# A one-core attention-and-MLP kernel: a quarter of w_out and one of w_in held behind a memset, six buffers for the last half tiles, and second stores right behind the first

## The chip, the cores and the metric

The kernel runs on one core of one Trainium2 chip. The metric is the device time of one execution in microseconds (us), the median over several runs. Before the change three runs gave 106.68, 106.97 and 108.76 us, median 106.97 us. Profiles come from one profiled execution each.

The engines are named as in the profile: PE (TensorE: matmuls; PEld is its weight load), DVE (VectorE), ACT (ScalarE), POOL (GpSimd) and SP (SyncE, which here only issues DMAs). SPq and ACTq are DMA issues on those two.

## The reference

An attention layer with polynomial sketch features is followed by a two-layer MLP with a PReLU that has one slope per hidden unit.

```python
def phi(x):                                   # 8 x 8 products of two 8-wide sketches
    a = np.einsum('rd,bhsd->bhsr', S1, x)
    b = np.einsum('rd,bhsd->bhsr', S2, x)
    return np.einsum('bhsi,bhsj->bhsij', a, b).reshape(*x.shape[:-1], r * r)
q_p, k_p = (phi(q), phi(k))
kv = np.einsum('bhsf,bhsd->bhfd', k_p, v)
z = np.sum(k_p, axis=2)
num = np.einsum('bhsf,bhfd->bhsd', q_p, kv)
den = np.einsum('bhsf,bhf->bhs', q_p, z)[..., None] + 1e-06
attn = num / den
x = attn.transpose(0, 2, 1, 3).reshape(B * S, H * D)
h = x @ w_in
out = (np.maximum(h, 0.0) + alpha * np.minimum(h, 0.0)) @ w_out
```

q, k and v are 4 batches x 4 heads x 1088 tokens x 32; r = 8; w_in is 128 x 2048, w_out 2048 x 128; the output is 4352 x 128, all float32.

## The kernel before, in words

The program is a graph of named operations that is written out in a fixed order. `Graph.build` makes the operations; the string `ORDER` lists them as `name@engine` (a, d, g, p, s for ACT, DVE, POOL, PE, SP), and every engine runs its own part of the list strictly in that order. The list `SLOTS` says which buffer of its class each temporary uses. No planner runs on the chip: an engine waits on semaphores for the data that its next instruction needs, and everything behind that instruction waits with it.

**Stages.** Loads bring q, k and v of the four batches and the weights in quarters (`w_in0`..`w_in3`, `w_out0`..`w_out3`, 256 KB each) into SBUF. For each batch the key side (`k{b}...`) builds features, products (`k0p00` and so on: batch 0, part 0 or 1, head 0 to 3) and the key-value matrix; the query side (`f0`, `f1` for the first 16 rows of batch 0, then `q0`..`q3`, `qr`) makes the normalised tokens x in bf16. The MLP then runs over tiles `0a`, `0b`, `1`..`9`: `h` is x @ w_in on PE into PSUM, `r` the ReLU on ACT or DVE, `o` the second matmul with `w_a` = (1 - alpha) w_out, and `W` adds x @ (w_in diag(alpha) w_out), because PReLU is (1 - alpha) ReLU(h) + alpha h.

**Weights.** From a quarter of w_out come `w_a{i}`, then `w_b{i}` (alpha times w_out, in one of two buffers, wb__111 and wb__112), then `w_hi{i}` and `w_lo{i}` (its bf16 head and rest). `Wmm` multiplies all of them with the transposed w_in on PE.

**Loads.** All large loads are issued by SP (line 143), in list order; a load that has to wait holds back those behind it. A `hold` operation (line 159) is a memset of one column of a load's destination: since the load writes the same column, its issue waits for the memset, which stands at a chosen place in another engine's order. There are eight DMA semaphores, used in turn, so a DMA also waits until the one eight places ahead of it has landed.

**The last tiles.** Tiles 1 to 6 hold 512 tokens; their result is transposed by DVE (`t1`..`t6`) into one of three oT buffers and leaves in two pairs of DMAs of 64 KB each (`s4.0`, `s4.1`). Tiles 7, 8 and 9 hold 256 tokens and end in halves a and b of 128: `t7a`..`t9b` copy PSUM to an oL buffer (ACT for the a halves, DVE for the b halves), and `s7a`..`s9b` store it from SP or ACT. All three a halves gather in the same PSUM bank, bank 7. The oL buffers are two tiles of their own (oL__101 and oL__102) and two old ones, E8 (printed as E) and kvF:

```python
T["oL"] += [T["E8"], T["kvF"]]
```

t7a and t8a use oL__101, t7b and t8b oL__102, t9b E8 and t9a kvF. The order of the last instructions is: `t8b` on DVE, then `t9b` on DVE; on ACT the issue of `s8a`, the issue of `s8b`, then `t9a` and the issue of `s9a`.

Of the kernel before, what the change touches and what calls it, by code (L numbers as in the profile page):

```python
# [42 lines left out]
class Graph:  # L43
# [106 lines left out]
    def loads(self):  # L150
        T = self.T
# [7 lines left out]
        hold = {n: self.op(f"hold.{n}", [("pool", 100, 140), ("dve", 60, 140)], lambda e, t=t: (self.nc.vector if e == "dve" else self.nc.gpsimd).memset(  # L159
            T[t][:, :1] if t != "q_r" else T[t][:, :1, :1], 0.0)) for n, t in (("k1", "k1"), ("q1", "q1"), ("k2", "k2"), ("q2", "q2"), ("qr", "q_r"))}  # L160
# [510 lines left out]
ld.k1.0@s f0.x@d q0cb@g vpad2@d fill@1 bit@2 h0a.6@p ld.k2.1@s f1.dT@d w_hi3@a ld.w_out2@s w_in_bf0@a h0a.4@p h0a.10@p r0a.6@a h0a.14@p w_lo3@g f1.e@a
k0W@a k1T0@d r0a.14@a w_b0@g winT0@p h0a.12@p q0s@d w_hi0@a winTc0@d f1.rc@d r0a.10@a q0e@a w_b2@g o0a.6@p k1f@p w_lo0@g winT1@p k1ab@d winTc1@d
w_hi2@a h0a.8@p h0a.2@p ld.q2.0@s ld.v3.3@s r0a.4@a r0a.8@a w_a0@a q0rc@d f1.num@p w_lo2@d q0bd@g f1.rr@d k1z@p r0a.12@d f1.x@d ld.q3.0@s ld.k2.0@s
q0p00@g q0p01@g k2T0@d h0a.0@p o0a.4@p Wmm@p h0b.4@p h0b.10@p r0a.0@a r0a.2@a o0a.0@p W_lo@a w_a2@g k1p01@g h0b.2@p W@d o0a.2@p W0a@p k1p00@g k1p03@g
k2f@p h0b.0@p o0a.8@p r0b.10@a q0t0@d k1zm@d w_a3@a o0a.10@p o0a.14@p r0b.0@a r0b.2@a k2ab@d ld.v2.1@s ld.qr@s ld.q1.0@s k1cw@p q0n@p q1T@d k1cc@d
q0x0@a q2T@d o0a.12@p h0b.12@p k2z@p t0a@d k2zm@d r0b.12@a r0b.4@a q1f@p h0b.14@p k1p02@g k2p00@g W0b@p o0b.2@p h1.6@p q1g@d q1cb@d ld.v1.1@s o0b.0@p
o0b.10@p h0b.6@p h1.13@p r0b.14@a r0b.6@a r1.6@a h1.9@p h1.5@p q1s@d k2p01@g ld.v1.2@s h0b.8@p h1.0@p ld.v1.3@s ld.v3.1@s ld.v2.3@s ld.v2.2@s
ld.v1.0@s q1e@g r0b.8@a o0b.4@p h1.10@p r1.5@a r1.9@a r1.10@a ld.v2.0@s ld.v3.0@s ld.k3.1@s h1.15@p r1.13@d q1rc@d h1.7@p o0b.14@p o0b.12@p h1.2@p
o0b.8@p h1.12@p r1.7@d k2p03@g q1bd@g o0b.6@p h1.4@p r1.2@d r1.15@a k2cw@p t0b@d k1v0@p k2cc@d r1.12@d r1.4@a q2f@p o1.12@p s0b.1@a k1vc@a h1.8@p
o1.5@p o1.4@p o1.6@p o1.15@p q1p00@g q1p01@g h1.3@p q2g@d W1@p h1.1@p o1.9@p h1.14@p r1.3@a q1p11@g k2p02@g ld.k3.0@s q1t0@d s0a.1@s h1.11@p k1vT@p  # L680
k2v0@p r1.0@a k1W@a r1.14@a k2vc@a r1.1@a q1p10@g q2cb@g o1.0@p o1.2@p q1t1@d r1.11@a k3T0@d r1.8@d q2s@d q2e@g o1.10@p o1.14@p o1.3@p o1.7@p q1n@p
q1x0@a k3f@p q2rc@d k3ab@d o1.8@p o1.1@p q1x2@a h2.6@p h2.8@p h2.11@p h2.2@p q2bd@g q2p00@g k3p01@g q2p01@g r2.8@a r2.6@a h2.3@p h2.0@p r2.3@a o1.13@p
o1.11@p h2.9@p r2.2@a r2.0@d t1@d h2.15@p k3z@p k2vT@p r2.9@d h2.14@p k3zm@d r2.14@d h3.10@p o2.2@p h2.1@p h3.2@p q2p11@g k3p00@g r2.11@a k2W@a qrT@d
r3.10@a q2p10@g k3p03@g r2.1@a r2.15@a h2.7@p o2.14@p h2.12@p o2.8@p h2.10@p h2.4@p o2.15@p o2.1@p ld.v3.2@s s1.1@s s0b.0@s r2.12@a r3.2@d o2.12@p
h3.3@p r2.4@a r2.10@a h3.13@p r2.7@a o2.9@p h2.13@p h2.5@p q3T@d o2.4@p o2.11@p o2.3@p h3.7@p W2@p h3.0@p o2.10@p q2t0@d h3.14@p r2.5@a r2.13@a r3.3@a
o2.13@p o2.6@p h3.11@p h3.9@p o2.0@p r3.13@d q2t1@d o2.5@p r3.7@a r3.0@a r3.9@a o2.7@p r3.14@a k3cw@p q2n@p t2@d r3.11@a k3cc@d q2x0@d q2x2@a h3.15@p
W3@p o3.14@p h3.5@p s1.0@s s0a.0@s q3f@p o3.3@p h4.14@p r3.15@d r3.5@a h3.6@p o3.10@p o3.11@p q3g@d o3.7@p h5.14@p h3.4@p o3.9@p h4.11@p h5.1@p q3cb@g
r3.4@a r4.14@d h3.8@p o3.5@p h4.1@p r5.1@a r4.11@a o3.0@p h3.1@p o3.13@p r3.6@d q3s@d r3.8@d q3e@g o3.2@p h3.12@p o3.4@p h4.9@p r3.12@a r5.14@d
k3p02@g r4.9@a r3.1@a h4.13@p h4.15@p q3rc@d o3.12@p o3.8@p o3.6@p h4.8@p h4.0@p o3.15@p h4.12@p h4.6@p o3.1@p r4.13@a q3bd@d r4.15@d t3@d r4.1@d
r4.8@a h4.2@p h4.7@p k3v0@p o4.9@p h4.4@p o4.1@p o4.15@p q3p11@g q3p10@g r4.7@a r4.2@a q3p00@d r4.4@a q3t1@d h5.3@p o4.8@p W4@p h5.13@p o4.4@p r4.12@a  # L690
k3vc@d q3p01@d r4.0@a h4.10@p h5.11@p o4.13@p h4.3@p o4.11@p r4.3@a o4.14@p o4.12@p r4.6@d q3t0@d h5.10@p h4.5@p o4.3@p o4.0@p r4.10@a r4.5@a s2.1@a
o4.7@p h5.5@p o4.2@p r5.10@d r5.13@d r5.5@d r5.3@a o4.6@p o4.5@p o4.10@p h5.15@p h5.6@p h5.4@p h5.2@p h5.9@p t4@d s2.0@s k3vT@p s4.1@s s3.1@s r5.9@d
r5.6@a r5.11@a r5.4@a o5.10@p o5.3@p o5.5@p o5.1@p k3W@d r5.15@d q3n@p q3x0@a h5.8@p h5.0@p r5.0@a o5.11@p q3x2@d o5.9@p qrf@p s3.0@a r5.8@a r5.2@d
qrg@d h6.6@p o5.6@p o5.15@p o5.0@p h5.12@p h5.7@p h6.10@p W5@p r5.7@d h6.5@p o5.4@p h6.9@p qrcb@g r5.12@d r6.9@d o5.7@p h6.15@p o5.13@p h6.12@p
o5.14@p o5.8@p r6.10@a r6.6@a qrs@d qre@d r6.15@a o5.12@p o5.2@p qrrc@d r6.12@d h6.2@p h6.3@p t5@d qrbd@g h6.14@p h6.13@p h8.12@p qrp00@g h6.1@p
r6.3@a r6.2@d r6.13@a r6.5@a o6.9@p o6.3@p h6.0@p o6.10@p s5.0@s r6.14@a r6.0@a o6.2@p h6.4@p h6.7@p o6.5@p o6.6@p r8.12@d qrt0@d r6.1@d o6.12@p qrn@p
qrx0@d o6.15@p h6.11@p r6.4@a o6.1@p h7.10@p h7.12@p h7.0@p h8.8@p r6.11@a r6.7@a o6.0@p h6.8@p r6.8@d r7.0@d o6.13@p r7.10@a o6.7@p h7.14@p h7.2@p
h7.4@p o7b.10@p W6@p r7.12@a o6.8@p o6.14@p o6.11@p o6.4@p r7.2@a r7.4@a o7b.4@p h8.2@p h9.10@p o7b.12@p r7.14@a t6@d r8.2@a h8.14@p h7.6@p r8.14@a
o7b.0@p h7.8@p s6.0@s o7a.12@p W7a@p o7a.10@p o7b.2@p o7a.4@p r7.8@d r8.8@d h9.8@p h8.0@p W7b@p o7a.2@p o7a.14@p r7.6@a o7a.6@p o7a.0@p o7a.8@p
o8b.8@p h9.2@p o8b.14@p h9.4@p r8.0@d r9.8@d t7a@a o8b.0@p o7b.8@p o7b.6@p h9.0@p o7b.14@p o8a.12@p r9.2@a s7a.0@s s4.0@s r9.10@d r9.0@d t7b@d W8a@p  # L700
h8.6@p o8a.14@p o8a.0@p h8.4@p r8.4@a s7b.0@s o8b.12@p h8.10@p r8.10@a h9.6@p W8b@p r9.4@a o8a.8@p o8b.2@p r8.6@d h9.12@p W9b@p o8a.2@p o8a.6@p
o8a.10@p o8a.4@p o8b.6@p o9b.8@p h9.14@p o9b.2@p s6.1@s s5.1@s r9.12@d t8a@a r9.6@a o9a.10@p o9a.8@p o9b.10@p o8b.4@p o9a.4@p W9a@p r9.14@d o9a.0@p
# [66 lines left out]
```

## Time and profile before

| what | value |
|---|---|
| runs (us) | 106.68, 106.97, 108.76; median 106.97 |
| profiled execution | 106.47 us; span 104.6 us from the first to the last instruction |
| granted TensorE clock | 0.991 |
| busy share: PE, DVE, ACT, POOL | 91%, 74%, 66%, 46% |
| data moved | 11.28 MB, HBM read 8.80 MB, written 2.23 MB |

A row of the chain of waits is a start, a length and what the time went to. A row of the timeline is a start, a length, the engine, the line of the kernel, the operation, output and inputs; xN merges N instructions, and a bracket gives the idle time of the engine before it and what ended that. A row of the windows gives a stretch, its length, and then busy time and instruction count for PE, PEld, DVE, ACT and POOL, the clock, the DMA engines' busy share and GB/s. L137 is the helper through which every matmul but the transposes is issued, and L134 the one for two-operand vector work, so tiles tell more than lines there.

### The profile page before, as it was taken

The numbers are of one execution on the slowest core, as the hardware profiler recorded it, in microseconds if no ns is written. First come the engines' busy times: TensorE is split into PE (matmuls) and PEld (weight loads), VectorE is DVE, ScalarE is ACT, GpSimd is POOL, SyncE is SP. The second block draws the span as 40 slices with busy tenths as digits, with TensorE's granted clock in tenths as the row PEclk, the third lists the DMA queues.
The fourth block names the chain that finished last, engine by engine and source line by source line (L and its number), as shares of the span: only waits on it lengthen the run. The fifth ranks groups of instructions, "written<-read, shape, count | busy, mean of one in ns | idle before, by whom it ended". The sixth has DMA issues, their size and how long they took to land.

```text
span 104.6 us, 3655 instructions
## 1 busy us (share of the span) xinstructions
PE 95.2 (91%) x1517; PEld 56.1 (54%) x1531; DVE 77.4 (74%) x149; ACT 68.5 (66%) x137; POOL 48.3 (46%) x65
## 2 busy tenths in 40 slices
PE   7998748999999999999999999999999999999920
PEld 2365626576766746444444444644534456699810
DVE  3589939999998686867986894999767963589510
ACT  3336994998769637479996279576566567855410
POOL 5169957989999996199910168000001500000000
PEclk9999999999999999999999999999999999999996
DMA  2997989999862100003502000002431020022362
GB/s 67 315 304 240 342 244 339 355 381 341 246 190 62 26 5 6 0 6 61 89 0 49 7 0 0 6 0 50 74 57 25 0 50 6 0 50 50 75 116 75
DMA packets 21730, 11.28 MB, mean 108 GB/s; under 512 B 16192, under 2 KB 19024, under 8 KB 21712
## 3 DMA queue, kind: packets, MB, share of 16 engines
q1 hardware_dynamic: 18552, 10.49, 34.9%
q10 hardware_dynamic: 3160, 0.54, 2.6%
q8 instruction: 12, 0.20, 0.8%
q14 instruction: 6, 0.05, 0.2%
HBM read 8.80 MB, written 2.23 MB: 105 GB/s over the span
## 4 chain that ended last, share of the span: by engine, by line
PE 75%; DMA 8%; SPq 5%; DVE 4%; issue 2%; ACT 2%; POOL 1%; ACTq 0%; DVEq 0%; POOLq 0%
PE ps L137 74%; DMA w_out_f<-in_moe_w_out_dram 5%; DMA out_dram<-oL__102 3%; SPq L578 3%; SPq L143 2%; POOL wb__112 L134 1%; DVE aq__82 L416 1%; DVE winT L124 1%; ACT w_hl L122 1%; DVE kp__70 L134 1%; DVE rh__91 L552 1%; ACT aq__82 L122 1%; PE ps L391 1%; DVE kvW L124 0%; ACTq L578 0%
## 5 line engine op out<-in xcount | busy, mean ns | idle before, releaser
L137 PE MATMUL ps<-xT__103,w_in_bf 128*128 128x512 bf16 (+1 forms) x111 | 28.0, 333 | 0.3 <-issue 0.2
L137 PEld LDWEIGHTS <-w_in_bf 128*128 128x128 bf16 x176 | 16.2, 98 | 12.6 <-issue 2.1
L137 PEld LDWEIGHTS <-w_a 128*128 128x128 bf16 x128 | 12.3, 98 | 12.6 <-issue 1.7
L137 PE MATMUL ps<-xT__104,w_in_bf 128*128 128x256 bf16 (+1 forms) x63 | 14.9, 326 | 0.1
L550 ACT ACTIVATE rh__88<-ps 128x512 bf16<-128x512 f32 x13 | 7.8, 597 | 7.0 <-PE ps L137 6.9
L550 ACT ACTIVATE rh__89<-ps 128x512 bf16<-128x512 f32 x15 | 9.0, 599 | 4.6 <-PE ps L137 4.6
L134 POOL TENSOR_TENSOR kp__69<-kab__66 128x576 f32<-128x576 f32 (+1 forms) x11 | 11.4, 1053 | 1.0 <-DVE kab__66 L333 0.9
L134 POOL TENSOR_TENSOR dn__80<-gt__73 128x128 f32<-128x128 f32 (+2 forms) x3 | 1.5, 498 | 22.0 <-DVE gt__73 L451 22.0
L550 ACT ACTIVATE rh__90<-ps 128x512 bf16<-128x512 f32 x12 | 7.1, 596 | 1.6 <-PE ps L137 1.1
L134 POOL TENSOR_TENSOR pr__75<-gt__73 128x512 f32<-128x512 f32 x7 | 7.3, 1068 | 0.7 <-DVE gt__73 L134 0.4
L323 DVE STREAM_TRANSPOSE kT__64<-k 128x1152 f32<-128x1152 f32 (+1 forms) x5 | 5.6, 1126 | 1.6 <-DMA k<-in_k_dram 1.4
L137 PE MATMUL ps<-const-bfloat16-1.0 128*128 128x512 bf16 (+1 forms) x20 | 5.8, 425 | 1.0 <-PEq L753 0.8
L137 PE MATMUL ps<-pt__78,kvW 32*32 32x256 f32 (+2 forms) x320 | 6.4, 332 | 0.1
L550 ACT ACTIVATE rh__92<-ps 128x512 bf16<-128x512 f32 x9 | 5.4, 602 | 1.3 <-PE ps L137 1.3
L552 DVE TENSOR_SCALAR rh__91<-ps 128x512 bf16<-128x512 f32 x7 | 4.7, 672 | 1.9 <-PE ps L137 1.6
L550 ACT ACTIVATE rh__93<-ps 128x512 bf16<-128x512 f32 x9 | 5.4, 601 | 0.8 <-PE ps L137 0.7
L550 ACT ACTIVATE rh__94<-ps 128x512 bf16<-128x512 f32 x9 | 5.4, 600 | 0.6 <-ACT rh__92 L550 0.4
L137 PE MATMUL ps<-rh__88,w_a 128*128 128x256 bf16 (+1 forms) x20 | 5.7, 326 | 0.1
L122 ACT CAST w_in_bf<-w_in_f 128x512 bf16<-128x512 f32 x4 | 4.5, 1122 | 1.7 <-DMA w_in_f<-in_moe_w_in_dram 1.7
L480 DVE STREAM_TRANSPOSE pt__78<-pr__75 128x1024 f32<-128x1024 f32 (+1 forms) x5 | 5.6, 1112 | 0.0
L137 PE MATMUL ps<-rh__89,w_a 128*128 128x512 bf16 (+1 forms) x16 | 5.3, 353 | 0.0
L137 PEld LDWEIGHTS ps<-pt__78,kvW 32*32 32x32 f32 x320 | 3.8, 103 | 2.3 <-DVE kvW L124 0.6
(199 smaller groups left out, 226.9 us busy)
## 6 DMA issues: line engine op xcount, KB each, us to landing
v<-in_v_dram SPq DMA_DIRECT2D x12, 144.0 KB, 3.9
q<-in_q_dram SPq DMA_DIRECT2D x3, 512.0 KB, 5.9
k<-in_k_dram SPq DMA_DIRECT2D x4, 288.0 KB, 4.5
k<-in_k_dram SPq DMA_DIRECT2D x4, 256.0 KB, 3.9
w_in_f<-in_moe_w_in_dram SPq DMA_DIRECT2D x4, 256.0 KB, 4.4
w_out_f<-in_moe_w_out_dram SPq DMA_DIRECT2D x4, 256.0 KB, 4.7
q<-in_q_dram SPq DMA_DIRECT2D x2, 256.0 KB, 4.2
out_dram<-oT__100 SPq DMA_DIRECT2D x8, 64.0 KB, 1.9
```

Of the source, the lines that this page charges most:

```text
L122: nc.scalar.copy(dst, src)
L124: (nc.vector if e == "dve" else nc.gpsimd).tensor_copy(dst, src)
L134: (self.nc.vector if e == "dve" else self.nc.gpsimd).tensor_tensor(out=dst, in0=a, in1=b, op=what)
L137: self.nc.tensor.matmul(out, w, x, start=start, stop=stop, skip_group_check=True)
L143: (self.nc.sync if eng == "sp" else self.nc.scalar).dma_start(dst(), src())
L323: turns.append(self.op(f"k{b}T{x}", [self.dvt(32 * NG * n)], lambda e, lo=lo, n=n: nc.vector.transpose(self.sb(bT, 32 * NG * lo, [1, 32 * ...
L391: nc.tensor.transpose(self.ps(bf4, 128 * f, [1, 128]), self.sb(bs4, 128 * f, [1, 128]), T["ident"])
L416: mu = self.op(f"f{u}.m", [self.dve(512)], lambda e, bp=bp, ba=ba: nc.vector.tensor_mul(self.sb(ba, 0, [128, 4], [1, 128]), self.ps(bp, 12 ...
L480: ts.append(self.op(f"{tag}t{x}", [self.dvt(64 * g)], lambda e, bP=bP, x=x: nc.vector.transpose(self.sb(bPT, 64 * g * x, [1, 64 * g]), sel ...
L550: nc.scalar.activation(self.sb(br), self.ps(bh, 0, [1, 512]), ACTF.Relu)
L552: nc.vector.tensor_scalar_max(self.sb(br), self.ps(bh, 0, [1, 512]), 0.0)
L578: (nc.scalar if e == "act" else nc.sync).dma_start(to(), at())
```

## The change

Four things are edited.

1. A new hold, `hold.wo`, clears one column of the fourth quarter of w_out (w_out_f3). It stands on POOL behind `k0p03`, and `ld.w_out3` depends on it.
2. In SP's order `ld.w_in1` goes ahead of `ld.w_out3`; `ld.w_in0` stays behind `ld.w_out3`, so it is held with it.
3. The class oL has six buffers instead of four: w_in_f0 and w_in_f1, whose contents were cast to bf16 near the start, join E8 and kvF. The slots of t8a, t8b, t9a, t9b move from oL__101, oL__102, kvF, E8 to E8, kvF, w_in_f0, w_in_f1. All six halves now have a buffer of their own.
4. The stores `s4.0`, `s5.1` and `s6.1` go directly behind `s4.1`, `s5.0` and `s6.0` on SP.

The diff, with the list of the order and the slots cut to the lines that carry this:

```diff
-               "rh": 10, "oT": 3, "oL": 4, "xT": 4, "zm": 2, "fs": 2, "wb": 2}
+               "rh": 10, "oT": 3, "oL": 6, "xT": 4, "zm": 2, "fs": 2, "wb": 2}
...
-            T[t][:, :1] if t != "q_r" else T[t][:, :1, :1], 0.0)) for n, t in (("k1", "k1"), ("q1", "q1"), ("k2", "k2"), ("q2", "q2"), ("qr", "q_r"))}
+            T[t][:, :1] if t not in ("q_r", "w_out_f3") else T[t][:, :1, :1], 0.0)) for n, t in (("k1", "k1"), ("q1", "q1"), ("k2", "k2"), ("q2", "q2"), ("qr", "q_r"), ("wo", "w_out_f3"))}
...
-                             lambda: self.dram("moe_w_out", 512 * i * DM, [512, 128], [1, 512]), 1 << 18, rate=420)
+                             lambda: self.dram("moe_w_out", 512 * i * DM, [512, 128], [1, 512]), 1 << 18, rate=420, deps=[hold["wo"]] if i == 3 else ())
...
-    T["oL"] += [T["E8"], T["kvF"]]
+    T["oL"] += [T["E8"], T["kvF"], T["w_in_f0"], T["w_in_f1"]]
...
-         4, 1, 6, 9, 2, 6, 3, 2, 1, 9, 6, 2, 7, 0, 5, 1, 0, 3, 3, 7, 2, 8, 0, 0, 6, 4, 4, 5, 4, 6, 6, 9, 7, 3, 1, 2]
+         4, 1, 6, 9, 2, 6, 3, 2, 1, 9, 6, 2, 7, 2, 5, 3, 0, 3, 3, 7, 2, 8, 0, 0, 6, 4, 4, 5, 4, 6, 6, 9, 7, 4, 1, 5]
```

SP's loads near the start, before (-) and now (+); w_in_f_150 to w_in_f_152 are w_in0 to w_in2, w_out_f_157 is w_out3, q_144 the second half of batch 0's q, and k_142 the second part of batch 1's k.

```order
 L143 DMA w_in_f_152<-in_moe_w_in_dram 128x512
 L143 DMA q_144<-in_q_dram 128x512
+L143 DMA w_in_f_151<-in_moe_w_in_dram 128x512
 L143 DMA w_out_f_157<-in_moe_w_out_dram 128x512
-L143 DMA w_in_f_151<-in_moe_w_in_dram 128x512
 L143 DMA w_in_f_150<-in_moe_w_in_dram 128x512
 L143 DMA k_142<-in_k_dram 128x512
```

w_in1 has moved ahead of w_out3; w_out3 now also waits for POOL, and w_in0 and the k load stand behind it as before.

SP's stores at the end, before (-) and now (+); oT__100, oT__98 and oT__99 hold tiles 4, 5 and 6, oL__101 and oL__102 the halves 7a and 7b.

```order
-L578 DMA out_dram<-oT__100 32x16x32 x2
-L578 DMA out_dram<-oT__98 32x16x32 x4
-L578 DMA out_dram<-oT__99 32x16x32 x2
+L578 DMA out_dram<-oT__100 32x16x32 x4
+L578 DMA out_dram<-oT__98 32x16x32 x6
+L578 DMA out_dram<-oT__99 32x16x32 x4
 L578 DMA out_dram<-oL__101 32x2x128 x2
-L578 DMA out_dram<-oT__100 32x16x32 x2
 L578 DMA out_dram<-oL__102 32x2x128 x2
-L578 DMA out_dram<-oT__99 32x16x32 x2
-L578 DMA out_dram<-oT__98 32x16x32 x2
```

The three late pairs, one between the stores of 7a and 7b and two behind them, have moved ahead of both.

ACT's last instructions, before (-) and now (+): the copies t8a and t9a (L122), the last ReLU of an even half tile (L550), and the issues of s8a, s8b and s9a (L578); E_128 is E8, w_in_f_150 is w_in_f0.

```order
 L550 ACTIVATE rh__90<-ps 128x512
 L550 ACTIVATE rh__96<-ps 128x512
-L122 COPY oL__101<-ps 128x128
+L122 COPY E_128<-ps 128x128
 L550 ACTIVATE rh__88<-ps 128x512
-L578 DMA out_dram<-oL__101 32x4x128
-L578 DMA out_dram<-oL__102 32x4x128
-L122 COPY kvF<-ps 128x128
+L578 DMA out_dram<-E_128 32x4x128
 L578 DMA out_dram<-kvF 32x4x128
+L122 COPY w_in_f_150<-ps 128x128
+L578 DMA out_dram<-w_in_f_150 32x4x128
```

The instructions and their order are the same; only the buffers differ, so t8a no longer writes the tile that s7a reads. On DVE the two last copies, t8b and t9b, likewise go to kvF and w_in_f1 instead of oL__102 and E8. PE's instructions are unchanged, and POOL has one memset more.

More of the change, by code (lines that the diff above doesn't have):

```diff
@@ L671 @@
[L671 to L702, printed above, removed]
@@ L703 @@
-o8b.10@p t8b@d o9b.0@p o9a.12@p o9b.14@p o9b.12@p o9b.4@p o9b.6@p s8a.0@a t9b@d s8b.0@a o9a.6@p s9b.0@s o9a.2@p o9a.14@p t9a@a s9a.0@a
+alphaT@d f0.a@p f0.b@p k0fz@p k0cw@p k0p00@g f0.ac@a w_a1@a w_in_bf2@a k0p10@d k0p03@g hold.wo@g f0.m@d fill@3 f1.a@p k0p02@d f1.b@p k0p13@g k0p12@g
+k0v0@p k0v1@p k0zz@d vpad1@d f1.ac@a k0cc@d kpad1@d k0zc@d k0Vc@a w_b1@g k0vc@a f0.den@p fill@1 k0VT@p ld.q0.1@s q0T1@d f1.m@d f0.dT@d hold.q2@d
+w_hi1@a f0.e@a k0V@d q0f@p ld.w_in1@s ld.w_out3@s k0vT@p f0.num@p f0.rc@d w_b3@g q0g@d ld.w_in0@s ld.k1.1@s ld.w_out0@s w_lo1@g f0.rr@d w_in_bf1@a
@@ new lines @@
+f1.den@p ld.k1.0@s f0.x@d q0cb@g vpad2@d fill@1 bit@2 h0a.6@p ld.k2.1@s f1.dT@d w_hi3@a ld.w_out2@s w_in_bf0@a h0a.4@p h0a.10@p r0a.6@a h0a.14@p
+w_lo3@g f1.e@a k0W@a k1T0@d r0a.14@a w_b0@g winT0@p h0a.12@p q0s@d w_hi0@a winTc0@d f1.rc@d r0a.10@a q0e@a w_b2@g o0a.6@p k1f@p w_lo0@g winT1@p k1ab@d
+winTc1@d w_hi2@a h0a.8@p h0a.2@p ld.q2.0@s ld.v3.3@s r0a.4@a r0a.8@a w_a0@a q0rc@d f1.num@p w_lo2@d q0bd@g f1.rr@d k1z@p r0a.12@d f1.x@d ld.q3.0@s
+ld.k2.0@s q0p00@g q0p01@g k2T0@d h0a.0@p o0a.4@p Wmm@p h0b.4@p h0b.10@p r0a.0@a r0a.2@a o0a.0@p W_lo@a w_a2@g k1p01@g h0b.2@p W@d o0a.2@p W0a@p
@@ new lines @@
+r8.2@a h8.14@p h7.6@p r8.14@a o7b.0@p h7.8@p s6.0@s s6.1@s o7a.12@p W7a@p o7a.10@p o7b.2@p o7a.4@p r7.8@d r8.8@d h9.8@p h8.0@p W7b@p o7a.2@p o7a.14@p
+r7.6@a o7a.6@p o7a.0@p o7a.8@p o8b.8@p h9.2@p o8b.14@p h9.4@p r8.0@d r9.8@d t7a@a o8b.0@p o7b.8@p o7b.6@p h9.0@p o7b.14@p o8a.12@p r9.2@a s7a.0@s
+r9.10@d r9.0@d t7b@d W8a@p h8.6@p o8a.14@p o8a.0@p h8.4@p r8.4@a s7b.0@s o8b.12@p h8.10@p r8.10@a h9.6@p W8b@p r9.4@a o8a.8@p o8b.2@p r8.6@d h9.12@p
+W9b@p o8a.2@p o8a.6@p o8a.10@p o8a.4@p o8b.6@p o9b.8@p h9.14@p o9b.2@p r9.12@d t8a@a r9.6@a o9a.10@p o9a.8@p o9b.10@p o8b.4@p o9a.4@p W9a@p r9.14@d
@@ L704 @@
+o9a.0@p o8b.10@p t8b@d o9b.0@p o9a.12@p o9b.14@p o9b.12@p o9b.4@p o9b.6@p s8a.0@a t9b@d s8b.0@a o9a.6@p s9b.0@s o9a.2@p o9a.14@p t9a@a s9a.0@a
 """
```

27 lines of the change are left out of this document (24 added, 3 removed).

## The prediction

> **What bounds the kernel now.** I read the page first, then the windows, the chain of waits, and the timeline at both ends.
>
> ```profile
> span 104.6 us, 3655 instructions
> PE 95.2 (91%) x1517; PEld 56.1 (54%) x1531; DVE 77.4 (74%) x149; ACT 68.5 (66%) x137; POOL 48.3 (46%) x65
> ```
>
> PE is idle for 104.6 - 95.2 = 9.4 us. The windows (stretch, length, then busy time and instructions of PE, PEld, DVE, ACT, POOL) tell where.
>
> ```profile
> 10.28:12.52 2.24, 2.21 (x120) 1.78 (x121) 1.98 (x8) 2.24 (x6) 2.24 (x4) 1.00 1.04 370
> 12.52:14.48 1.96, 0.00 (x0) 0.00 (x0) 0.80 (x3) 1.89 (x5) 1.95 (x2) 1.00 0.87 271
> 26.00:90.00 64.00, 63.17 (x967) 33.66 (x978) 50.13 (x82) 44.69 (x87) 29.06 (x32) 1.00 0.19 42
> ```
>
> From 26 to 90 us PE is idle for 0.83 us of 64, and its instructions don't change. An edit can gain there only by reaching those 0.83 us; what it can gain besides lies at the two ends. One hole at the start is 1.96 us in which PE does nothing at all. The chain, at the start and at the end:
>
> ```profile
> 13.90 5.02 DMA w_out_f<-in_moe_w_out_dram
> ...
> 19.05 1.05 POOL wb__112 L134
> ...
> 21.46 9.65 PE ps L137 x196
> ...
> 97.31 3.13 DMA out_dram<-oL__102
> ...
> 100.51 0.29 DVE oL__102 L124
> ...
> 101.43 0.27 ACT kvF L122
> ```
>
> The start hangs, by this chain, on a quarter of w_out that lands at 13.90 + 5.02 = 18.92 us. The end hangs on a store: the DMA that reads oL__102 (s7b) lands at 97.31 + 3.13 = 100.44, and 0.07 us later DVE copies the next half, t8b, into the same buffer. That is the place where the change takes something away for certain.
>
> **The end: six buffers.** PE's last matmuls, the first rows for the wait before 97.95:
>
> ```profile
> 97.54 0.28 PE L137 MATMUL ps<-w_a,rh__95 128*128 128x128 bf16 x2
> 97.95 0.27 PE L137 MATMUL ps<-w_a,rh__93 128*128 128x128 bf16 x2
> ...
> 98.67 0.28 PE L137 MATMUL ps<-w_a,rh__90 128*128 128x128 bf16 x2
> ...
> 99.34 0.39 PE L137 MATMUL ps<-w_a,rh__88 128*128 128x128 bf16 x4
> ...
> 99.68 0.28 PE L137 MATMUL ps<-w_a,rh__97 128*128 128x128 bf16 x2
> ```
>
> By the written order the 98.67 row is o8b.10, the last matmul of half 8b; the 99.34 row holds o9b.6, the last of 9b; the 99.68 row is o9a.14, the last of all. What ACT and DVE then do:
>
> ```profile
> 97.63 0.27 ACT L122 COPY oL__101<-ps 128x128 f32<-128x128 f32 x1 [0.34 <-ACT rh__96 L550]
> ...
> 97.93 0.66 ACTq L578 DMA_DIRECT2D out_dram<-oL__101  x1
> 100.84 0.55 ACTq L578 DMA_DIRECT2D out_dram<-oL__102  x1
> 101.43 0.27 ACT L122 COPY kvF<-ps 128x128 f32<-128x128 f32 x1 [3.03 <-DVE E L124]
> 101.72 0.55 ACTq L578 DMA_DIRECT2D out_dram<-kvF  x1
> ```
>
> ```profile
> 100.51 0.29 DVE L124 COPY oL__102<-ps 128x128 f32<-128x128 f32 x1 [2.09 <-DMA out_dram<-oL__102]
> 100.72 0.28 DVE L124 COPY E<-ps 128x128 f32<-128x128 f32 x1
> ```
>
> Half 8b is ready at 98.67 + 0.28 = 98.95, but t8b starts at 100.51. Behind it wait t9b on DVE and, on ACT, the issue of s8b (100.84) and t9a (101.43), which stands behind that issue though PE had finished at 99.68 + 0.28 = 99.96.
>
> With its own buffer t8b runs at 98.95 + 0.07 = 99.02 (the 0.07 as between the store's landing and t8b in the chain) to 99.31. s8b is issued 0.04 later, as before (100.80 to 100.84), and takes 0.55: 99.90. t9a needs ACT and PE: 99.90 + 0.04 or 99.96 + 0.07 = 100.03, so 100.03 instead of 101.43, a gain of 1.40 us. The issue of s9a keeps its distance of 0.29 to t9a. t9b needs the 99.34 row, whose end is 99.73 at the latest: 99.80 to 100.08 and its store is issued by SP ahead of s9a. What is late next is PE itself.
>
> A smaller term: PE stands still from 97.54 + 0.28 = 97.82 to 97.95. The matmul at 97.95 opens half 9a in bank 7, which t8a empties until 97.90. t8a had ACT idle for 0.34 us before it; in the order it waits for the two stores of s7a, since it writes oL__101. It now writes E8 and can start at 97.29, so these 0.13 us of PE go too, and all that follows moves. If ACT had waited there for something else, this term is nothing. Sum at the end: 1.40 + 0.13 = 1.53 us. The last store itself should land as fast:
>
> ```profile
> out_dram<-kvF ACTq DMA_DIRECT2D x1, 64.0 KB, 1.9
> ```
>
> **The stores that move.** On SP these stood between and behind the stores of tile 7:
>
> ```profile
> 95.08 1.13 SPq L578 DMA_DIRECT2D out_dram<-oT__100  x2
> 96.72 1.45 SPq L578 DMA_DIRECT2D out_dram<-oL__102  x2
> ```
>
> Without the first pair s7b is issued earlier, but with six buffers nobody waits for s7b any more, so I count no second gain. The pairs now go out before 94 us, while PE has work that no store feeds: about 1.1 us of SP each, SP idle otherwise. Cost and gain nothing. If this cover fails, s7a is issued up to 1.1 us later, and that only reaches t8a through a buffer that it no longer uses.
>
> **The start: the held loads.**
>
> ```profile
> 7.41 0.43 SPq L143 DMA_DIRECT2D w_out_f<-in_moe_w_out_dram  x1
> 7.89 0.90 SPq L143 DMA_DIRECT2D w_in_f<-in_moe_w_in_dram  x2
> 11.37 0.33 SPq L143 DMA_DIRECT2D k<-in_k_dram  x1
> ```
>
> ```profile
> 1.32 0.10 POOL L159 MEMSET q_r<- 128x1 f32 x1
> ...
> 8.05 1.86 POOL L134 TENSOR_TENSOR kp__70<-kab__66 128x320 f32<-128x320 f32 x2
> ...
> 12.29 1.04 POOL L134 TENSOR_TENSOR wb__112<-w_out_f,alphaT 128x512 f32<-128x512 f32 x1
> 13.34 1.16 POOL L134 TENSOR_TENSOR w_hl<-wb__111,w_hl 128x512 bf16<-128x512 f32 x1
> 16.23 0.46 POOL L134 TENSOR_TENSOR dn__80<-gt__73 128x128 f32<-128x128 f32 x1 [1.73 <-DVE gt__73 L451]
> ```
>
> The memset is POOL's next instruction behind the two kp__70 products, which end at 8.05 + 1.86 = 9.91. Like the memset at 1.32 it takes at most 0.10 us, so w_out3 is issued at about 10.0 instead of 7.41 and w_in0 at about 10.5; w_in1 takes the place at 7.41. Both issues end by 10.9, and the next load, k of batch 1, was issued only at 11.37, so SP's later loads keep their times. The 0.10 us on POOL are covered by the 1.73 us of idle time before 16.23; without that cover they cost 0.10.
>
> When does w_out3 land? The nearest rows, for the first load (an empty queue) and for the slowest quarter of w_out:
>
> ```profile
> k<-in_k_dram SPq DMA_DIRECT2D x1, 288.0 KB, 2.9
> ...
> w_out_f<-in_moe_w_out_dram SPq DMA_DIRECT2D x1, 256.0 KB, 5.0
> ```
>
> So between 12.9 and 15.0. Its first user is w_b3, the 12.29 row; behind it on POOL are w_lo1 (1.16) and then a wait for DVE until 16.23. w_b3 and w_lo1 need 1.04 + 1.16 = 2.20 us, so a landing until 16.23 - 2.20 = 14.0 costs nothing. I take about 13.3, nearer to the empty queue, because the two loads ahead of it (q and w_in1) were issued over 2 us before. On ACT:
>
> ```profile
> 14.44 0.62 ACT L122 CAST w_hl<-wb__112 128x512 bf16<-128x512 f32 x1
> ...
> 17.47 0.60 ACT L550 ACTIVATE rh__88<-ps 128x512 bf16<-128x512 f32 x1 [1.39 <-PE ps L137]
> ```
>
> w_hi3 at 14.44 needs w_b3, which ends at 13.3 + 1.04 = 14.34: nothing. At 15.0 it would slip to 16.1, by 1.7 us, with w_in_bf0 and the first ReLU behind it; 1.39 us are covered by ACT's idle time before 17.47, leaving 0.3. POOL would be 15.0 - 14.0 = 1.0 us late. So the hold's cost lies between nothing and 1.0. The other way, no load ahead of it waits behind it, so w_in1 alone is earlier, and nothing waited for w_in1. I take zero.
>
> The Trainium skill, "DMA: Bandwidth & Descriptors", section Rules for kernel authors, says to issue a DMA early and wait for it late; by that rule the hold gives away 2.6 us of cover and is a loss. The trace so far bears out only that the cover shrinks; this is the second rival below, with its price there.
>
> **Sum.** 106.47 - 1.53 = 104.9 us for the profiled execution. That execution was below all three runs; with 106.68 and 106.97 it has a mean of 106.7, and 106.7 - 1.53 = **105.2 us** is the forecast. Against the median 106.97 the same sum gives 105.4.
>
> **Rivals.** *PE's hole at 12.52 shrinks (the larger gain).*
>
> ```profile
> PE ps L382 <- ACT dt__84 L129: 2.0, 1, 2.0
> ```
>
> ```profile
> q8 instruction: 1, 0.02, 4.6%
> ```
>
> The waits blame ACT, but in the order the transpose at L382 needs only an ACT copy that stands ahead of dt__84. The DMA view of 12.0 to 13.2 shows one transfer of an instruction queue, and PE had just run 120 matmuls and 121 weight loads in 2.24 us (the window's row): it may be out of instructions. The edit takes 512 KB out of the queue between 7.4 and 10 us, so this fetch could meet less traffic. Against it: the two loads are there again from about 12. The whole hole is 1.96 us; half of it gives 105.2 - 1.0 = 104.2, all of it 103.2. The Trainium skill, "Runtime: NRT & Kernel Launch", section Instruction fetch mechanics, calls such refills mostly hidden; by that page this rival has nothing to gain. No row here decides it.
>
> *The hold costs what its upper bound says.* Landing at 15.0, POOL 1.0 us late: 105.2 + 0.3 to 105.2 + 1.0 = 105.5 to 106.2. For it: the landing of 5.0 us is in the trace. Against it: the queue is shorter then.
>
> *The six buffers don't shorten the end.* The last store may be limited by something that the trace hides behind the buffer wait, such as slower stores. The store of 3.13 us shows that they vary; 3.13 - 1.9 = 1.2 of the 1.53 us would be lost: 106.4.
>
> *Slower: the queue runs dry.* If the 2.6 us of later issue become 2.6 us of empty DMA engines, all loads behind are that much later, also the quarter that lands at 18.92 on the chain; then PE's 21.46 moves with it: 106.7 - 1.53 + 2.6 = 107.8. It decides from a slip of 1.53 us on. Against it: SP itself stood still until 11.37, so the later loads were not queued up against the held ones.
>
> **How the numbers follow.** Chances: forecast 0.55, hole shrinks 0.20, hold costs 0.14, no shorter end 0.05, queue dry 0.06. Two per cent of 106.97, about what a measurement of this kernel tells from no change, is 2.1 us, so faster means below 104.8. Of the hole's 0.20 about 0.17 lie there, and 0.05 of the forecast's own spread (the base is known to 0.3): 0.22. Slower by over 2% needs more than 109.1, that is a slip of 3.9 us, the dry queue and more besides: 0.04. The rest, 0.74, is within 2%. The range reaches from most of the hole, 103.9, to the no-gain cases, 106.7.
>
> **What would show it.** Right: t8b starts within 0.1 us of half 8b's last matmul, its wait for a DMA is gone from the waits, t9a starts about 0.1 us after PE's last matmul and the span ends about 3 us behind that. The chain's end has no DMA of an oL tile ahead of t8b. POOL's w_b3 starts between 12.9 and 14.0 with ACT's 14.44 row unmoved. Wrong: w_b3 after 14.0, PE's hole longer or shorter than 1.96 us, PE's last matmul away from 99.8, or a last store of 3 us.

## The result and the profile after

| | runs | median (lowest to highest), us |
|---|---|---|
| before | 20 | 108.06 (106.39 to 109.19) |
| after | 20 | 105.84 (104.78 to 108.63) |

The ratio is 0.9848, 95% interval 0.981 to 0.9886: the change makes the kernel 1.1 to 1.9% faster. Here and below, medians are over all executions of a kernel, and ratios over those within 1.5% of its fastest. The forecast was 1.53 of 106.7 us, or 1.4%.

The profile that came with the result happens to be of the slowest execution (108.63 us), in which PE ran at half clock for 3.4 us; the rows of "after" below are therefore of another profiled execution of the same kernel, 105.55 us, from the last series of experiments. Its page:

```profile
span 103.8 us, 3668 instructions
PE 97.3 (94%) x1531; PEld 56.3 (54%) x1531; DVE 77.5 (75%) x149; ACT 68.7 (66%) x137; POOL 48.3 (47%) x66
```

PE's idle time must not be compared with the 9.4 us of before: that page has records of 1517 of the 1531 matmuls (PEld has all 1531), this one has all. The first series of experiments has a trace of the whole change with 1517 records, and there PE is idle for 103.8 - 95.3 = 8.5 us. The timeline of its end (start, length, engine, line, operation; in brackets the idle time before and what ended it), PE's last row first, then ACT, DVE and SP:

```profile
100.32 0.28 PE L137 MATMUL ps<-w_a,rh__97 128*128 128x128 bf16 x2
...
98.24 0.27 ACT L122 COPY E<-ps 128x128 f32<-128x128 f32 x1
98.53 0.64 ACTq L578 DMA_DIRECT2D out_dram<-E  x1
99.95 0.55 ACTq L578 DMA_DIRECT2D out_dram<-kvF  x1
100.63 0.27 ACT L122 COPY w_in_f<-ps 128x128 f32<-128x128 f32 x1 [1.63 <-PE ps L137]
100.93 0.55 ACTq L578 DMA_DIRECT2D out_dram<-w_in_f  x1
...
99.63 0.29 DVE L124 COPY kvF<-ps 128x128 f32<-128x128 f32 x1 [0.26 <-PE ps L137]
100.30 0.29 DVE L124 COPY w_in_f<-ps 128x128 f32<-128x128 f32 x1 [0.38 <-PE ps L137]
...
94.73 1.25 SPq L578 DMA_DIRECT2D out_dram<-oL__101  x2
96.91 1.18 SPq L578 DMA_DIRECT2D out_dram<-oL__102  x2
100.62 0.57 SPq L578 DMA_DIRECT2D out_dram<-w_in_f  x1
```

t8b (99.63) now waits 0.26 us for PE, where it waited 2.09 for a store; t8a (98.24) has no wait; t9a (100.63) starts 0.03 us after PE's last matmul (100.32 + 0.28 = 100.60), where it started 1.47 us after it. The chain of waits ends without a DMA:

```profile
75.84 24.77 PE ps L137 x331
100.61 0.02 issue
100.63 0.27 ACT w_in_f L122
```

At the start, PE, DVE and POOL of the same execution, in the places that the prediction names:

```profile
10.89 0.10 POOL L159 MEMSET w_out_f<- 128x1 f32 x1
13.64 1.04 POOL L134 TENSOR_TENSOR wb__112<-w_out_f,alphaT 128x512 f32<-128x512 f32 x1 [0.23 <-DMA w_out_f<-in_moe_w_out_dram]
...
13.49 0.39 PE L137 MATMUL ps<-const-bfloat16-1.0 128*128 128x512 bf16 x1
13.84 0.33 PE L382 MATMUL ps<-ident,fs__109 128*128 128x128 f32 x1
20.09 0.72 PE L137 MATMUL ps<-kT__64,kW 64*32 64x288 f32 x16 [1.77 <-DVE kT__64 L323]
...
18.66 1.38 DVE L323 STREAM_TRANSPOSE kT__64<-k 128x1152 f32<-128x1152 f32 x1 [1.73 <-DMA k<-in_k_dram]
```

Two things happened there. The hole of 1.96 us in front of the transposes at L382 is gone (13.49 + 0.39 = 13.88, and the next row starts at 13.84). Some 0.4 us of that hole was work all along: the 13.49 row is a fill matmul, and in the trace of before only its weight load has a record (at 12.42). And a hole of 1.77 us stands further on, before the matmuls on kT__64: DVE transposes the first part of batch 1's k only when its load lands (18.66, after a wait of 1.73). Before the change that wait was not there:

```profile
17.72 1.38 DVE L323 STREAM_TRANSPOSE kT__64<-k 128x1152 f32<-128x1152 f32 x1
19.15 0.72 PE L137 MATMUL ps<-kT__64,kW 64*32 64x288 f32 x16 [0.18 <-DVE kT__64 L323]
```

### The profile page after: what moved, and what is told of

Its sections match the earlier page's. It is cut to its first block, busy times and chain, and to the rows that moved or that the text cites. A ratio compares the mean times of both kernels' runs of the same rounds, so it can differ in the third digit from the quotient of the medians.

```text
span 106.9 us, 3654 instructions
## 1 busy us (share of the span) xinstructions
PE 96.9 (91%) x1517; PEld 56.8 (53%) x1531; DVE 78.2 (73%) x149; ACT 69.0 (65%) x137; POOL 48.0 (45%) x66
## 4 chain that ended last, share of the span: by engine, by line
PE 76%; DVE 10%; DMA 6%; ACTq 1%; issue 1%; ACT 1%; SPq 1%; DVEq 0%
PE ps L137 75%; DMA k<-in_k_dram 6%; ACTq L578 1%; DVE kT__64 L323 1%; DVE gt__73 L451 1%; DVE dn__80 L134 1%; PE ps L299 1%; SPq L143 1%; DVE rh__97 L552 1%; DVE aq__82 L416 1%; DVE kp__70 L134 1%; DVE rh__89 L552 1%; DVE qT__71 L512 1%; DVE rh__96 L552 1%; DVE rh__91 L552 1%
## 5 line engine op out<-in xcount | busy, mean ns | idle before, releaser
L137 PE MATMUL ps<-xT__103,w_in_bf 128*128 128x512 bf16 (+1 forms) x111 | 28.6, 339 | 0.8 <-DVE rh__96 L552 0.2
L550 ACT ACTIVATE rh__89<-ps 128x512 bf16<-128x512 f32 x15 | 9.0, 600 | 4.6 <-PE ps L137 4.6
L550 ACT ACTIVATE rh__88<-ps 128x512 bf16<-128x512 f32 x13 | 7.8, 598 | 5.5 <-PE ps L137 5.2
L550 ACT ACTIVATE rh__90<-ps 128x512 bf16<-128x512 f32 x12 | 7.2, 596 | 2.2 <-PE ps L137 1.1
L137 PE MATMUL ps<-kT__64,kW 64*32 64x288 f32 x64 | 3.4, 482 | 3.4 <-DVE kT__64 L323 3.4
L550 ACT ACTIVATE rh__92<-ps 128x512 bf16<-128x512 f32 x9 | 5.4, 603 | 1.3 <-PE ps L137 1.3
L550 ACT ACTIVATE rh__93<-ps 128x512 bf16<-128x512 f32 x9 | 5.4, 602 | 0.6 <-PE ps L137 0.5
L550 ACT ACTIVATE rh__94<-ps 128x512 bf16<-128x512 f32 x9 | 5.4, 601 | 0.6 <-ACT rh__92 L550 0.4
L122 ACT CAST w_in_bf<-w_in_f 128x512 bf16<-128x512 f32 x4 | 4.5, 1127 | 1.9 <-DMA w_in_f<-in_moe_w_in_dram 1.9
```

What stands on the lines that cost most here:

```text
L122: nc.scalar.copy(dst, src)
L137: self.nc.tensor.matmul(out, w, x, start=start, stop=stop, skip_group_check=True)
L550: nc.scalar.activation(self.sb(br), self.ps(bh, 0, [1, 512]), ACTF.Relu)
```

## The experiments

The theory after the result: the gain is made at the end, by buffers and stores together, and the hold gains nothing. The rivals: the buffers do it alone; the hold has a share, through PE's first hole. Every series of runs had its own runs of the kernel before beside it (30, 17 and 17 of them, medians 107.12, 107.6 and 107.22 us).

**One part at a time.** `e1_end_only`: the six buffers alone.

```diff
-    T["oL"] += [T["E8"], T["kvF"]]
+    T["oL"] += [T["E8"], T["kvF"], T["w_in_f0"], T["w_in_f1"]]
```

> Only the six buffers of the change: no held load, no moved load, stores where they were. If the gain comes from the end alone (the recorded forecast), the time is about 1.4 us under the kernel before (ratio 0.987), t9a starts within 0.1 us of PE's last matmul, and PE's hole before the transpose at L382 stays near 2 us. If the gain needs the earlier start of PE, the ratio stays above 0.993. Since s6.1 and s5.1 still stand behind s7b on SP here, s9b could be issued up to 1 us late; then the end moves by less, about 0.5 us.

`e2_hold_only`: the hold and the place of w_in1 alone.

```diff
-q0f@p ld.w_out3@s k0vT@p f0.num@p f0.rc@d w_b3@g q0g@d ld.w_in1@s ld.w_in0@s
+q0f@p ld.w_in1@s ld.w_out3@s k0vT@p f0.num@p f0.rc@d w_b3@g q0g@d ld.w_in0@s
-k0p03@g
+k0p03@g hold.wo@g
...
+                             deps=[hold["wo"]] if i == 3 else ())
```

> Only the held w_out3 and w_in0, with w_in1 ahead of them. If the hold is worth nothing (the forecast), the ratio is 0.997 to 1.003. If it shortens PE's hole before L382 and that reaches the end, the hole falls from 2.0 us to about 0.7 us and the time by up to 1.3 us (ratio down to 0.988). If the later landing of w_out3 costs, POOL's w_b3 starts after 14.0 us and the ratio is 1.003 to 1.010.

`e3_end_stores`: buffers and moved stores, no hold.

```diff
+    T["oL"] += [T["E8"], T["kvF"], T["w_in_f0"], T["w_in_f1"]]
...
+s4.1@s s4.0@s
+s5.0@s s5.1@s
+s6.0@s s6.1@s
```

> The change without its hold: six buffers and the three second stores right behind the first ones. If the stores cost and gain nothing, the time is within 0.2 us of the run with the six buffers alone, ratio 0.985 to 0.988. If the stores matter because s9b no longer stands behind s6.1 and s5.1 on SP, this run is 0.3 to 1.0 us faster than that one.

`e4_full`: the whole change again.

> The whole change once more, on the same chip as its parts, for a profile of its usual state. If the parts add up with a hold that is worth nothing, it equals the run without the hold within 0.2 us. If the hold gains, it is 0.5 to 1.3 us faster than that run, and its PE hole before L382 is near 0.7 us.

`e5_stores_only`: the moved stores alone, with the four buffers of before.

```diff
+s4.1@s s4.0@s
+s5.0@s s5.1@s
+s6.0@s s6.1@s
...
-s7a.0@s s4.0@s
+s7a.0@s
...
-s6.1@s s5.1@s
```

> Only the three second stores right behind the first ones; four buffers, no hold. t8b still waits for the store of half 7b, but that store no longer stands behind the second pair of tile 4 on SP: it is issued when t7b is done, about 96.0 instead of 96.7 us by the profile of before, so t8b, t9a and the end can come up to 0.75 us earlier, ratio 0.993. If the moved stores are worth nothing without the buffers, the ratio is 0.998 to 1.002.

| kernel | median, us (runs) | ratio to before, 95% interval |
|---|---|---|
| six buffers alone | 107.09 (12) | 0.9967, 0.9926 to 1.0008 |
| moved stores alone | 107.16 (12) | 0.9919, 0.985 to 0.9987 |
| both | 105.51 (6) | 0.9872, 0.9828 to 0.9915 |
| hold alone | 107.81 (12) | 1.0029, 0.997 to 1.0088 |
| whole change | 106.78 (12) | 0.9897, 0.9859 to 0.9935 |

The buffers alone gain no more than can be measured. Their timeline shows why; SP's last rows and ACT's last:

```profile
99.81 1.61 SPq L578 DMA_DIRECT2D out_dram<-oT__99  x2
101.47 1.12 SPq L578 DMA_DIRECT2D out_dram<-oT__98  x2
102.69 0.57 SPq L578 DMA_DIRECT2D out_dram<-w_in_f  x1
...
101.60 0.55 ACTq L578 DMA_DIRECT2D out_dram<-w_in_f  x1
```

t9b was done at 100.97 + 0.29 = 101.26, but its store is the last row of SP and goes out at 102.69, behind four stores of tiles 6 and 5. ACT had issued the other last store at 101.60. With the stores moved and the old buffers:

```profile
94.20 1.25 SPq L578 DMA_DIRECT2D out_dram<-oL__101  x2
96.38 1.17 SPq L578 DMA_DIRECT2D out_dram<-oL__102  x2
...
97.95 0.28 PE L137 MATMUL ps<-w_a,rh__95 128*128 128x128 bf16 x2
98.05 0.27 ACT L122 COPY oL__101<-ps 128x128 f32<-128x128 f32 x1 [0.34 <-ACT rh__96 L550]
98.36 0.27 PE L137 MATMUL ps<-w_a,rh__93 128*128 128x128 bf16 x2
...
99.40 0.29 DVE L124 COPY oL__102<-ps 128x128 f32<-128x128 f32 x1 [0.56 <-PE ps L137]
```

the pair of s7b is issued directly behind t7b and has landed (at 98.89) before t8b needs oL__102, although the buffer is shared: t8b waits for PE. But this execution is the fastest of its twelve (105.33 us), and part of it is luck. The time from issue to landing of s7b's second store is, with the moved stores alone and then in the whole change:

```profile
out_dram<-oL__102 SPq DMA_DIRECT2D x2, 32.0 KB, 1.9
```

```profile
out_dram<-oL__102 SPq DMA_DIRECT2D x2, 32.0 KB, 3.4
```

By the landings in the traces, of ten with the moved stores four have 1.9 to 2.2 us, and six have 2.8 to 3.8. In those six s7b lands 0.7 to 1.7 us after t8b has started on a buffer of its own (in the whole change at 100.91, t8b at 99.63). With the old buffers t8b would have waited for it there, so the six buffers are what makes t8b independent of that store. The moved stores alone save the wait only where s7b lands fast. No second execution of them was profiled, and their median of 107.16 us against 107.6 leaves room for both kinds.

In every one of the following traces the span ends 2.8 to 2.9 us behind the issue of the last store, so the end can be measured as the time from PE's last matmul to that issue:

| profiled execution | PE ends | last store issued | difference |
|---|---|---|---|
| before | 99.96 | 101.72 | 1.76 |
| six buffers alone | 101.28 | 102.69 | 1.41 |
| moved stores alone | 100.37 | 100.70 | 0.33 |
| both | 99.87 | 100.20 | 0.33 |
| whole change | 100.60 | 100.93 | 0.33 |

So in these executions the stores alone take 1.43 us off the end, the buffers alone 0.35, and together they take the same 1.43. Besides t8b's independence the buffers add PE's gap of 0.13 us in front of half 9a: it is still in the trace of the stores alone (97.95 + 0.28 = 98.23 to 98.36) and in neither of the last two.

**PE's first hole.** `e7_more_small_matmuls`: the kernel with buffers and stores; one warm-up step on PE has 24 small matmuls instead of 6 large ones, so PE gets 36 instructions more ahead of the hole (a matmul and its weight load count as two).

```diff
-fill@6 S1x@p
+bit@24 S1x@p
```

> Six buffers and moved stores, no hold, and of the warm-up the six 512-column matmuls are replaced by 24 of 128 columns, the same columns in all: 36 PE instructions more ahead of the hole, with no other dependence. If the hole is PE out of instructions at a fixed count, it moves 36 instructions ahead in the program: it then opens before or within the 32 instructions of f0.den (aq__82 with zc), not at the transpose at L382, and PE goes on about 2.3 us after the instruction queue's transfer starts. If the hole is a wait of the transpose for ACT, it stays directly ahead of L382.

Measured: 106.31 us (4 runs), ratio 0.9819 (0.9708 to 0.993). PE's rows:

```profile
14.04 0.24 PE L137 MATMUL ps<-kp__69,v 128*32 128x64 f32 x1 [1.63 <-issue]
14.21 0.45 PE L137 MATMUL ps<-aq__82,zc 64*32 64x128 f32 x16
14.91 0.33 PE L382 MATMUL ps<-ident,fs__109 128*128 128x128 f32 x1 [0.25 <-ACT fs__110 L122]
```

The hole has left L382, where only 0.25 us remain, and stands ahead of the last matmul on kp__69, with nothing that PE waits for. By the program's order that is 18 matmuls earlier (one on kp__69, 16 on aq__82, one fill), and 18 matmuls with their weight loads are the 36 instructions. The traces agree: wherever there is a hole, PE has 221 weight loads behind it when it stops. So the hole belongs to a count of instructions, not to a datum. What PE waits for is, by the times, the transfer of 16 KB on the instruction queue (q8 in the page): in every trace with such a hole PE goes on 2.2 to 2.4 us after that transfer begins.

**The hold against the hole, and its dose.** `e6_late_hold` is the whole change with the memset further on in POOL's order, behind w_b1:

```diff
-k0p03@g hold.wo@g f0.m@d
+k0p03@g f0.m@d
-w_b1@g k0vc@a
+w_b1@g hold.wo@g k0vc@a
```

> The whole change with the hold doubled: the memset stands behind w_b1 on POOL, so that w_out3 and w_in0 are issued about 2.4 us later (near 12.5 us), and k of batch 1 behind them at about 13.4 instead of 11.5 us. If the hold costs through what is queued behind it (k of batch 1, then the transpose k1T0 and PE's k1f), PE's second hole, before k1f, grows by 1.2 to 1.9 us and the ratio is 1.00 to 1.01. If the hold is free, the ratio stays at 0.985 to 0.991.

`e8_k1_first` is the kernel with buffers and stores, with the load of the first part of batch 1's k moved ahead of that of w_out0.

```diff
-ld.k1.1@s ld.w_out0@s w_lo1@g f0.rr@d w_in_bf1@a f1.den@p ld.k1.0@s
+ld.k1.1@s ld.k1.0@s ld.w_out0@s w_lo1@g f0.rr@d w_in_bf1@a f1.den@p
```

> Six buffers and moved stores, no hold, and the second load of k of batch 1 (k1.0) goes ahead of w_out0 on SP. If PE's second hole, before k1f, comes from the landing of k1.0, k1T0 starts up to 0.7 us earlier in runs with a short first hole, and the ratio is 0.982 to 0.987. If w_out0, now later, holds w_b0 on POOL instead, nothing is gained: ratio 0.987 to 0.992.

The profiled execution of the late hold took 322.3 us, with every matmul stretched, and is of no use; the other five had 107.28 to 110.19 us. k1 first had 105.36 us (6 runs), ratio 0.9806 (0.9728 to 0.9883). These two, the whole change and the kernel without the hold were then run once more together on one chip:

> The whole change again, on one chip with the two kernels that follow. If the held quarter of w_out costs what the profiled executions show (the weights behind it land later, k1.0 by some 0.5 us, and the matmuls on kT__64 wait for k1.0), this kernel stands 0.2 to 0.4% above the one that has the six buffers and the moved stores without the hold, at a ratio of 0.985 to 0.990. If the hold is free, the two agree within 0.1%.

> Six buffers and moved stores, no hold. Ratio 0.984 to 0.988 if the hold costs 0.2 to 0.4%; the same as the whole change if the hold is free; above the whole change if the hold gains something that single profiles hid.

> As the kernel before it, with the load of k1.0 ahead of that of w_out0 on its queue. If the wait for k1.0 is what ends PE's second hole, that hole goes and the time falls by 0.3 to 0.7% against the same kernel without the move; if w_out0, then landing later, is waited for in its place, nothing is gained.

> The whole change with a larger dose of the hold: the memset that releases the quarter of w_out stands behind w_b1 on GpSimd, so the load starts later still. If the hold costs by its queue (all loads behind it land later), PE's hole ahead of the matmuls on kT__64 grows by 1 to 2 us, and the ratio is 1.00 to 1.02. If the hold costs nothing, the ratio stays at 0.985 to 0.99.

| kernel | median, us (runs) | ratio, 95% interval |
|---|---|---|
| whole change | 105.56 (6) | 0.9846, 0.9784 to 0.9908 |
| without the hold | 105.47 (6) | 0.9857, 0.98 to 0.9914 |
| without the hold, k1.0 first | 106.2 (12) | 0.9801, 0.9751 to 0.985 |
| whole change, later hold | 109.71 (6) | 1.0166, 1.0069 to 1.0262 |

With and without the hold the medians differ by 0.09 us. The expected cost of 0.2 to 0.4% isn't there; nor is a gain. The first series is less kind to the hold: 106.78 us with it against 105.51 without, and 107.81 for the hold alone against 107.12 before. Six of the twelve executions of the whole change took 106.75 to 107.16 us there, at a clock of 1.00, and five 105.16 to 105.90. The twelve executions of buffers and stores have eleven at a clock of 0.995 or more, and none of these is above 106.32. No trace of such an execution was taken, so a cost of about 1.3 us in some executions is open; a gain by the hold shows in no series. PE's and DVE's rows of the kernel without the hold:

```profile
14.49 0.33 PE L382 MATMUL ps<-ident,fs__109 128*128 128x128 f32 x1 [1.10 <-ACT dt__84 L129]
18.91 0.71 PE L137 MATMUL ps<-kT__64,kW 64*32 64x288 f32 x16
...
17.51 1.33 DVE L323 STREAM_TRANSPOSE kT__64<-k 128x1152 f32<-128x1152 f32 x1
```

Here the first hole is there (1.10) and the second isn't. All profiled executions of these kernels, with the start of the 16-KB transfer as the trace's records of q8 have it (a hole under 0.2 us is not printed in the timeline and stands as 0):

| execution | hold | transfer starts | PE goes on | first hole | second hole |
|---|---|---|---|---|---|
| before | no | 12.13 | 14.48 | 1.99 | 0.18 |
| six buffers alone | no | 13.06 | 15.42 | 2.14 | 0 |
| moved stores alone | no | 11.97 | 14.26 | 1.23 | 0 |
| buffers and stores | no | 11.61 | 13.82 | 0.96 | 0.98 |
| the same, last series | no | 12.21 | 14.49 | 1.10 | 0 |
| hold alone | yes | 11.90 | 14.25 | 1.41 | 0.80 |
| whole, with the result | yes | 11.12 | 13.29 | 0.66 | 3.38 |
| whole, first series | yes | 10.98 | 13.36 | 0.74 | 1.71 |
| whole, last series | yes | 10.62 | 13.84 | 0 | 1.77 |

Without the hold the first hole averages 1.48 us and the second 0.23; with it 0.70 and 1.92. (The rows of the last series have the fill matmul's record, the others lack it. Measured alike, up to the end of the matmuls on aq__82, the last series has 1.42 and 0.28, and the averages are 1.55 and 0.77.) The first hole is 0.8 us shorter and the second 1.7 longer, so the hold's traces lose more than they gain. With the hold the transfer starts earlier than in any execution without it, but for one (11.90), so PE's instructions come earlier; then PE meets the wait for k1.0, whose load now lands later. The DMA share tells what stands between: the windows of 11 to 12 us, the whole change first, the kernel without the hold second (the two numbers at the end are the DMA share and GB/s).

```profile
11.00:12.00 1.00, 0.80 (x37) 0.52 (x38) 1.00 (x3) 1.00 (x4) 1.00 (x2) 1.00 0.19 59
```

```profile
11.00:12.00 1.00, 1.00 (x68) 0.83 (x68) 1.00 (x7) 1.00 (x2) 1.00 (x3) 1.00 1.03 381
```

SP waits for the memset, the DMA engines run nearly empty for most of a microsecond, and the bytes that weren't moved then are missing later. This is the extreme case: in the other three traces with the hold the same window has a share of 0.75 to 0.85, at 215 to 242 GB/s. The transfer of instructions starts at 10.62, ahead of the empty stretch, so the empty engines aren't what starts it; why it starts earlier with the hold wasn't isolated.

The later hold shows the same with a larger dose, the windows first:

```profile
12.00:14.00 2.00, 2.00 (x113) 1.38 (x96) 1.74 (x8) 2.00 (x5) 1.69 (x3) 1.00 0.00 0
```

```profile
13.59 0.10 POOL L159 MEMSET w_out_f<- 128x1 f32 x1
16.46 1.04 POOL L134 TENSOR_TENSOR wb__112<-w_out_f,alphaT 128x512 f32<-128x512 f32 x1 [2.77 <-DMA w_out_f<-in_moe_w_out_dram]
...
20.16 1.00 PE L299 MATMUL ps<-identb,w_in_bf 128*128 128x128 bf16 x8 [2.44 <-ACT w_in_bf L122]
22.48 1.22 PE L137 MATMUL ps<-kT__64,kW 64*32 64x288 f32 x16 [0.47 <-DVE kT__64 L323]
```

No byte moves for 2 us, PE's first hole is gone here too, and PE instead waits 2.44 us for w_in0, which is held behind w_out3, and 0.47 for k1.0. The kernel is slower than before by 0.7 to 2.6%. That is not the price of the loads alone: all six executions have a mean clock of 0.953 to 0.984, and the profiled one runs at half clock for 3.41 us behind the hole of 2.44. The one execution of this kernel at full clock, in the series before, took 107.28 us, where the kernel before had a median of 107.6. The expectation had the hole in front of kT__64; its larger part came one group of matmuls earlier, at w_in0.

k1 first does remove the second hole (21.45, no wait), yet gains nothing sure: its rows have a first hole of 2.57 us, and then a stretch at half clock (the second window; the 0.50 is the clock):

```profile
15.51 0.33 PE L382 MATMUL ps<-ident,fs__109 128*128 128x128 f32 x1 [2.57 <-ACT w_in_bf L122]
21.45 0.71 PE L137 MATMUL ps<-kT__64,kW 64*32 64x288 f32 x16
```

```profile
14.22:17.63 3.41, 1.91 (x68) 0.96 (x69) 1.47 (x5) 2.55 (x4) 1.25 (x2) 1.00 1.02 328
17.63:21.04 3.41, 3.41 (x28) 2.58 (x22) 2.40 (x6) 1.82 (x5) 3.19 (x4) 0.50 0.99 364
21.04:24.46 3.42, 3.27 (x70) 1.94 (x69) 2.91 (x7) 3.34 (x10) 1.68 (x2) 1.00 1.01 328
```

Its executions without such a stretch have a median of 105.25 us, against 105.47 for the kernel without the move, but 6 of its 12 had one and the median over all is 106.2. Hold and k1 first together, which by the table would have neither hole, were not run.

## Why the prediction was right, and where it wasn't

**The end, in size right.** The sum was 1.53 us. The last store's issue moved from 1.76 to 0.33 us behind PE (1.43), and PE's gap of 0.13 is gone: 1.56. t8b, t9b and t9a wait for PE, and PE is what is late next, as the prediction had it. ACT's wait of 0.34 us before t8a is still there with the old buffers and the moved stores (the 98.05 row) and gone with six buffers, so it hung on the buffer that s7a reads, as the step said. It was no wait for the landing of s7a, though: that came at 96.75, and in the trace of before at 96.34, about 1 us before the idle time began. What the 0.34 us are stays open.

**The stores that move: the step failed.** The prediction gave the whole 1.53 us to the buffers and wrote of the stores "Cost and gain nothing". In the profiled executions the buffers alone are worth 0.35 us at the end, and the stores alone 1.43. The step that failed is "its store is issued by SP ahead of s9a": it holds only if the two later pairs are out of the way. Without that the store of t9b is issued 1.09 us (102.69 - 101.60) behind ACT's, and the kernel ends with it. The moved stores have a second effect: s7b no longer stands behind the first moved pair on SP, and where it then lands in 2 us the shared buffer doesn't matter either. Where it lands in 3.4 us the buffers are needed, as the prediction had it. So each of the two edits takes away a wait that the other may leave. The sum came out because both are in the change; that the stores were in it, though priced at nothing, is luck.

**The hold: zero, by another route.** The prediction had it free because w_out3 would land by 14.0 and SP's later loads keep their times. w_b3 started at 13.64 in the profile above, at 13.91 in the first series and at 14.54 with the hold alone, so the bound was partly missed. ACT's row of 14.44, which was to stay, moved to 15.50, 14.99 and 15.62, and harmlessly: the first ReLU, at 17.47 before, started at 17.05, 16.55 and 17.24. What the step left out is the loads behind. Their issues moved little, but the k load was waited for until 18.66, where the kernel without the hold had it before 17.51. In the traces that costs 1.7 us, of which the shorter first hole gives back 0.8; in the medians the hold costs between nothing and 1.3 us. Zero was the lower end of the prediction's own bounds, not a measured size.

**The rival of PE's hole: half right.** The hole is a fetch of instructions and it does shrink under the hold, by about 0.8 us on average over the traces. The time of 104.2 us was wrong since the next wait, for k1.0, took it back. The prediction's signs of being wrong (a hole away from 1.96 us, PE's last matmul away from 99.8) did come: the holes are 0 to 0.74, and the last matmul starts at 100.32. PE reached its end 0.64 us later than in the trace of before. Two readings were off from the start: the 9.4 us of PE's idle time, and the hole in which PE "does nothing at all", hold matmuls that have no record, some 0.4 us of them in the hole. The Trainium skill, "Runtime: NRT & Kernel Launch", section Instruction fetch mechanics, which the prediction weighed, calls these refills mostly hidden; here PE has a hole of 0.7 to 2.1 us in eight of the nine executions of the table (the fill matmul's 0.4 us included in most), and the measurement decides.

**The other rivals.** The end did shorten. The dry queue happened for most of a microsecond in one trace, below the slip of 1.53 us from which it was to decide; with the later hold it went past that point, and the kernel lost its gain and, at the reduced clock, more. That is the direction in which the rule of the Trainium skill, "DMA: Bandwidth & Descriptors", section Rules for kernel authors (issue early, wait late), points; at the dose of this change it costs nothing that 0.9846 against 0.9857 can show, and perhaps something in the first series.

**The absolute time** came out 0.6 us above the forecast, 105.84 to 105.2, and that nearness is partly luck. The base of 106.7 was drawn from three executions: twenty gave 108.06, the later series 107.1 to 107.6. From 108.06 the sum would have given 106.5. The medians fell by 2.2 us instead of 1.53; part of that may be the clock, which in the later series was under 0.985 in fewer executions with the change (last section).

## What to carry to other kernels

When a copy waits for a store that reads its buffer, there are two cures, another buffer and an earlier issue of that store; look on the issuing queue for what stands ahead of it, and test each cure alone before giving it the gain. Look at more than one trace of it, since the landing of one and the same store took from 1.9 to 3.8 us here. When a hole on the critical engine closes, read off which datum of its next instructions lands last, since that is what the engine meets next. A load that is held back empties the queue for all loads behind it, so follow the one that is waited for, not the one that is held.
